# Batch 0 by quarters of the spectrum, `x` in rows of six, and one form of gate: a fused 2-D DFT and gated feed-forward on one Trainium2 core

## The chip, the cores and the metric

The kernel runs on one core of one Trainium2 chip. Five engines work from in-order queues of their own: TensorE (PE, with weight loads shown as PEld), VectorE (DVE), ScalarE (ACT), GpSimd (POOL) and SyncE (SP), which issues most transfers. The core has 16 DMA engines. The metric is the device time of one execution in microseconds (us); lower is better.

## The reference, cut to what matters

```
x: (8, 3008, 256) f32            # batch, sequence, channel
X = fft(fft(x, axis=1), axis=2).real          # (8, 3008, 256)
x = X.reshape(24064, 256)
gate = maximum(x @ w_gate, 0)                 # w_gate: (256, 1536)
val  = x @ w_val                              # w_val:  (256, 1536)
out  = (gate * val) @ w_out                   # w_out:  (1536, 256), out f32
```

## The kernel before

**The mathematics on the chip.** The transform along the channels is folded into the weights: `weights(c, ...)` multiplies cosine and sine tables (TA, TB) with `w_gate` (index 0) and `w_val` (index 1) and leaves WA, WB and WM in bf16, WM being WB with its mirror's sign and weight. The transform along the sequence is done for each batch as products with tables: tabC and tabS hold cosines and sines of six chunks of up to 128 sequence positions. By symmetry the input is first folded: row s is added to its mirror S - s with reversed channels (`fold_a`, `fold_a0`), the two halves of the sequence are added and subtracted (`fold_pq`, giving PQ, families 0 and 1), and the channels are folded to F (cosine part) and G (sine part) (`fold_f`, `fold_f0`, `fold_g`). XD holds rows in ascending order, XG their mirrors, which are gathered by index with indirect DMAs from POOL (`load_mirror`, six gathers of up to 128 pairs of rows); `load_rows` loads XD with six plain DMAs of 128 or 120 rows of two sequence positions, and two small ones. F and G times the tables give U and V, spectrum by columns: 4 x 376 + 1 columns for a batch.

**Feed-forward tiles.** A tile is one block of columns by 128 of the 1536 hidden features (12 tiles to a block). Both signs of the frequency come from the same U and V: WA and U plus WB and V give one sign, and adding WM and V gives its mirror. Each tile leaves h in bf16 for both signs, and blocks of h times `wo` give rows of the output (`out_steps`: for batches 1 to 7 96 products of 256 columns in each block), which go through ACT (os) to DRAM by DMAs from SP.

**Batch 0** is worked in four blocks ("segments") of 376 or 377 columns, and everything is set up around it: tables for odd frequencies on DVE and ACT, weights chunk 0, the fold of the batch on DVE (lines 303 to 312), the first transform `dft_first`, then the first block's 12 tiles (`first_tile`), with weights of chunks 1 and 2 between them, and then segments 1 to 3 (`single_tile`). POOL reduces the arguments of the even tables (`even_rest`), gathers batch 1's mirrors, and folds batches 1 and 2 (`fold_steps`, run before segments 2 and 3). The whole odd family (two segments) is transformed before the first tile, the even family during segment 1, and batch 1 in segments 2 and 3.

**Batches 1 to 7** have three blocks ("thirds") of 504, 504 and 497 columns, 36 slots to a batch (`slot`). While the tiles of batch b run, POOL folds batch b + 2, paced by a credit (`run_fold(fold_us)`, with costs written beside each step), and PE transforms batch b + 1 at slots written out by hand (`DFT_EVEN`, `DFT_ODD`). A tile is of one of two kinds. Kind "o" is computed with six products (two gate, gate mirror, two value, value mirror). Kind "n" takes five: the sine part of the gate in a product (`sine_part`, L689), copied out by ACT (L692); channel 128's share put into PSUM by ACT (`seed`, L684) and the cosine part added to it (`cosine_part`, L696); one sum on DVE (L700) and one on POOL (L701) give both signs. The rule is:

```python
st["kind"] = "o" if b < 6 and fi % (6 if b < 2 else 12) == 5 else "n"
```

which makes 6 tiles of batch 1 and 3 each of batches 2 to 5 of kind "o", 18 in all. Channel 128 of a batch goes through DRAM (`ch128`) and comes back by two DMAs on SP: `row_128` (all partitions of CB) and `row_0` (row 0 of V), queued with the transform's steps 6 and 21 in batch 0.

**Order.** Instructions are issued in the order in which the program emits them, each engine and each DMA queue in order; an instruction that waits holds what is behind it on its engine. DMAs from SP and ACT take eight semaphores in turn.

## Time and profile before

| | |
|---|---|
| median of 3 runs | 647.61 us (647.56 to 647.71) |
| the profiled execution | 647.91 us, its span 646.1 us |
| PE, PEld | 620.9 us (96%), 401.6 us (62%) busy |
| DVE, ACT, POOL | 543.7 us (84%), 450.6 us (70%), 535.5 us (83%) busy |
| first product on PE; first gate product | 16.0 us; 24.4 us |
| first output product of batch 1; of batch 2 | 113.3 us; 188.5 us |
| L701, POOL's sums for "n" tiles | 234 of 1252 ns |
| L102, gathers of mirrors | 48 of 1017 ns |
| granted clock of PE | 1.00 |

Times in the trace count from the span's start. A line L496 is line 496 of the kernel; a group "out<-in" names the tile written and those read. The share of busy time is a mean over stages with different limits, so stages are looked at one by one.

### The profile page before, as it was taken

The page shows a single profiled execution, that of the slowest core. Times are in us where ns is not written, and L with a number is a line of the kernel's source. Part 1 is how long each engine was busy: PE and PEld are TensorE (multiplying, and loading weights), DVE is VectorE, ACT ScalarE, POOL GpSimd, SP SyncE. Part 2 cuts the span into 40 slices and gives each one's busy share as a digit, 9 for nine tenths or more (in the row PEclk, how much of TensorE's full clock was granted, in tenths as well). Part 3 has the DMA queues.
Part 4 walks back from the last instruction along what each step waited for, and adds up shares of the span by engine and source line. Part 5 has one row for each costly group of instructions (what it writes and reads, how often), then busy time and mean ns, then how long its engine had stood idle before and what let it go on. Part 6 is the DMA issues. An engine that isn't in the chain of part 4 may idle for free.

```text
span 646.1 us, 12223 instructions
## 1 busy us (share of the span) xinstructions
PE 620.9 (96%) x4160; PEld 401.6 (62%) x4160; DVE 543.7 (84%) x970; ACT 450.6 (70%) x822; POOL 535.5 (83%) x593
## 2 busy tenths in 40 slices
PE   0999999999999999999999999999999999999996
PEld 0356676566666666666666666666666666666665
DVE  8875566887888899898998889988899899999990
ACT  8697666767666776777677677676777767777751
POOL 8589997899999999999899999999876656666660
PEclk9999999999999999999999999999999999999999
DMA  8922544224332433241222422311211111111112
GB/s 227 207 67 64 178 127 137 62 68 145 89 83 63 127 98 90 64 136 58 89 84 78 129 73 82 93 35 49 73 34 49 44 62 49 35 48 49 50 49 79
DMA packets 42438, 55.24 MB, mean 85 GB/s; under 512 B 5153, under 2 KB 32353, under 8 KB 42376
## 3 DMA queue, kind: packets, MB, share of 16 engines
q1 hardware_dynamic: 34552, 39.23, 19.7%
q0 software_dynamic: 7536, 14.72, 9.3%
q8 instruction: 32, 0.52, 0.4%
q10 hardware_dynamic: 288, 0.52, 0.2%
q14 instruction: 30, 0.25, 0.1%
HBM read 32.14 MB, written 24.67 MB: 88 GB/s over the span
## 4 chain that ended last, share of the span: by engine, by line
PE 69%; DVE 12%; POOL 9%; issue 6%; ACT 3%; DMA 0%; DVEq 0%; SPq 0%; ACTq 0%; POOLq 0%
PE o L496 27%; PE v L575 7%; PE v L570 7%; PE v L571 7%; DVE h L597 6%; PE g L689 5%; PE p L696 5%; DVE r L700 5%; POOL r L701 4%; PE d L385 4%; PE p L575 1%; POOL XG L113 1%; POOL PQ L121 1%; POOL XG L102 1%; PE p L571 1%
## 5 line engine op out<-in xcount | busy, mean ns | idle before, releaser
L701 POOL TENSOR_TENSOR r<-r 128x504 f32<-128x504 f32 (+1 forms) x234 | 291.7, 1252 | 73.8 <-DVE r L700 72.3
L496 PE MATMUL o<-wo,h 128*128 128x256 bf16 x2304 | 342.3, 273 | 0.0
L597 DVE SCALAR_TENSOR_TENSOR h<-r,v 128x504 bf16<-128x504 f32 (+1 forms) x468 | 297.3, 673 | 51.1 <-PE v L575 37.8
L496 PEld LDWEIGHTS <-h 128*128 128x128 bf16 x2304 | 225.2, 98 | 114.7 <-issue 2.3
L684 ACT ACTIVATE p<-CB,b 128x504 f32<-128x504 bf16 (+1 forms) x234 | 160.0, 684 | 55.3 <-DVE r L700 52.8
L692 ACT COPY r<-g 128x504 f32<-128x504 f32 (+1 forms) x234 | 135.0, 577 | 58.6 <-PE g L689 54.5
L700 DVE SCALAR_TENSOR_TENSOR r<-r,p 128x504 f32<-128x504 f32 (+1 forms) x234 | 156.7, 670 | 0.6 <-ACT r L692 0.6
L575 PE MATMUL v<-V,WM 128*128 128x504 bf16 (+3 forms) x296 | 108.6, 367 | 1.6 <-DVE h L597 1.0
L570 PE MATMUL v<-U,WA 128*128 128x504 bf16 (+3 forms) x296 | 108.6, 367 | 0.1
L571 PE MATMUL v<-V,WB 128*128 128x504 bf16 (+3 forms) x296 | 108.7, 367 | 0.0
L593 DVE TENSOR_TENSOR h<-r,v 128x376 bf16<-128x376 f32 (+3 forms) x124 | 68.9, 580 | 25.7 <-PE v L575 13.6
L689 PE MATMUL g<-V,WM 128*128 128x504 bf16 (+1 forms) x234 | 87.8, 375 | 0.5 <-ACT r L692 0.3
L696 PE MATMUL p<-U,WA 128*128 128x504 bf16 (+1 forms) x234 | 87.8, 375 | 0.0
L502 ACT COPY os<-o 128x512 f32<-128x512 f32 x96 | 55.7, 580 | 14.5 <-PE o L496 8.1
L570 PEld LDWEIGHTS <-WA 128*128 128x128 bf16 x366 | 35.7, 98 | 38.3 <-issue 8.9
L571 PEld LDWEIGHTS <-WB 128*128 128x128 bf16 x366 | 35.7, 98 | 35.7 <-ACT WB L291 0.7
L102 POOL DMA_INDIRECT XG<-in_x_dram,gidx x48 | 48.8, 1017 | 8.7 <-issue 6.3
L113 POOL TENSOR_TENSOR XG<-XG,XD 128x510 f32<-128x510 f32 x42 | 52.5, 1265 | 0.1
L585 ACT ACTIVATE r<-g 128x504 f32<-128x504 f32 (+3 forms) x48 | 27.3, 569 | 35.0 <-PE g L571 31.8
L585 ACT ACTIVATE r<-p 128x376 f32<-128x376 f32 (+1 forms) x80 | 38.2, 490 | 18.7 <-PE p L575 10.9
L121 POOL TENSOR_TENSOR PQ<-XG 128x510 f32<-128x510 f32 x42 | 45.0, 1091 | 0.0
L575 PEld LDWEIGHTS <-WM 128*128 128x128 bf16 x366 | 35.8, 98 | 11.4 <-issue 0.2
(127 smaller groups left out, 430.4 us busy)
## 6 DMA issues: line engine op xcount, KB each, us to landing
out_dram<-os SPq DMA_DIRECT2D x118, 128.0 KB
XD<-in_x_dram SPq DMA_DIRECT2D x30, 256.0 KB
out_dram<-os SPq DMA_DIRECT2D x62, 120.0 KB
XD<-in_x_dram SPq DMA_DIRECT2D x16, 240.0 KB
CB<-ch SPq DMA_DIRECT2D x7, 376.2 KB
out_dram<-os SPq DMA_DIRECT2D x10, 127.0 KB
XG<-in_x_dram,gidx POOLq DMA_INDIRECT x48
h<-in_moe_w_gate_dram POOLq DMA_DIRECT2D x3, 256.0 KB
```

The source lines that it names most:

```text
L496: nc.tensor.matmul(st["p"][:, q, :], lhsT=hs[f][:, sign, h0:h0 + 128], rhs=wo[:, f, :], start=(f == 0), stop=(f == NF - 1))
L570: nc.tensor.matmul(bank[:, 0:st["n"]], lhsT=WA[i][:, st["f"]], rhs=st["us"], start=True, stop=False)
L571: nc.tensor.matmul(bank[:, 0:st["n"]], lhsT=WB[i][:, st["f"]], rhs=st["vs"], start=False, stop=True)
L575: nc.tensor.matmul(bank[:, 0:st["n"]], lhsT=WM[i][:, st["f"]], rhs=st["vs"], start=False, stop=True, skip_group_check=True)
L593: nc.vector.tensor_tensor(half_h(st, sign), (r or st["r"])[:, 0:n], st["v"][:, 0:n], op=ALU.mult)
L597: nc.vector.scalar_tensor_tensor(half_h(st, sign), in0=st["s"][1 + sign][:, 0:n], scalar=0.0, in1=st["v"][:, 0:n], op0=ALU.max, op1=ALU.mult)
L684: nc.scalar.activation(st["p"][:, 0:st["n"]], st["c"], ACTF.Copy, scale=b2[:, st["fi"]:st["fi"] + 1])
L689: nc.tensor.matmul(st["g"][:, 0:n], lhsT=WM[0][:, st["f"]], rhs=st["vs"], start=True, stop=True)
L692: nc.scalar.copy(q[:, 0:n], st["g"][:, 0:n])
L696: nc.tensor.matmul(st["p"][:, 0:n], lhsT=WA[0][:, st["f"]], rhs=st["us"], start=False, stop=True, skip_group_check=True)
L700: nc.vector.scalar_tensor_tensor(sp[:, 0:n], in0=q[:, 0:n], scalar=-0.5, in1=st["p"][:, 0:n], op0=ALU.mult, op1=ALU.add)
L701: nc.gpsimd.tensor_tensor(sm[:, 0:n], sp[:, 0:n], q[:, 0:n], op=ALU.add)
```

## The change

Six things are changed together.

- **`x` in rows of six.** XD and XG hold six consecutive rows of `x` in a partition and use 126 partitions (NP): 125 with six rows each, and a last one filled by five small DMAs (`load_ends`; in batch 0 after a DMA of zeros to that partition). `load_rows` is two DMAs of 125 rows of 6 KB a batch (six DMAs of 125 rows of 2 KB in batch 0, three on SP's queue and three on ACT's), mirrors are two gathers of 125 rows of 6 KB instead of six. The fold now adds XG into XD, so XD is loaded for the next batch after `fold_pq` and not after `fold_a`; `fold_pq` takes all 256 channels at once.
- **Batch 0 in quarters.** Columns are ordered so that each block of 376 columns needs only 188 columns of the tables (`QUARTERS`). Before the first tile only quarter 0's tables are made and transformed; the tables of quarter 1 are reduced on POOL, of quarter 2 on POOL, of quarter 3 on DVE (`vector_rest`), the sines follow on ACT between the tiles, and each quarter is transformed during the block before it.
- **Fold of batch 0**: DVE does family 1 only; POOL does family 0 in `pool_goes_on`, called in the ninth tile of block 0, and then loads batch 1 and gathers its mirrors.
- **Weights** in four parts of 256, 384, 384 and 512 features (`PARTS`) instead of three of 512; WB is copied by DVE and WM of the last two parts made by POOL.
- **All tiles of batches 1 to 7 are of kind "n".** `run_fold` gets 0.8 in place of 1.1 (batch 1) or 0.9.
- **Order in batch 0**: the folds of batches 1 and 2 are queued from the eighth tile of block 1 at 2.0 a tile (`FOLD_0`); the transform of batch 1 is all in block 3, `row_128` with its step 6 and `row_0` with step 18.

```diff
-    ROWS = {0: (128, 128, 120), 1: (128, 128, 121)}
+    NP = 126
+    ROWS = {0: (NP, NP - 1, NP - 1), 1: (NP, NP, NP - 1)}
...
+    PARTS = ((0, 256), (256, 384), (640, 384), (1024, 512))
...
+    def load_rows(b, ts=slice(0, 3), queue=None):
+        o, (ks, _) = b * S * D, at(ts)
+        for r in range(2):
+            (queue if queue and r else nc.sync).dma_start(out=D6[0:NP - 1, r, ks],
+                                                         in_=dram(x, o + (1 + ks.start + r * H) * D, [[6 * D, NP - 1], [D, ks.stop - ks.start], [1, D]]))
+
+    def load_ends(b, own=True, mirror=True):
+
         o = b * S * D
...
+        last = slice(NP - 1, NP)
+        if own:
+            nc.sync.dma_start(out=D6[last, 0, 0:2], in_=dram(x, o + 751 * D, [[0, 1], [D, 2], [1, D]]))
+            nc.sync.dma_start(out=D6[last, 1, 0], in_=dram(x, o + (H + 751) * D, [[0, 1], [1, D]]))
+            nc.sync.dma_start(out=D6[last, :, 3], in_=dram(x, o, [[0, 1], [H * D, 2], [1, D]]))
+        if mirror:
+            nc.sync.dma_start(out=G6[last, 0, 4:6], in_=dram(x, o + (S - 752) * D, [[0, 1], [D, 2], [1, D]]))
+            nc.sync.dma_start(out=G6[last, 1, 5], in_=dram(x, o + (H - 751) * D, [[0, 1], [1, D]]))
...
+    def fold_a(e, p, r, ts):
+        ks, js = at(ts)
+        e.tensor_tensor(D6[p, r, ks, 1:D], D6[p, r, ks, 1:D], G6[p, r, js, D - 1:0:-1], op=ALU.add)
...
+    def fold_pq(e, p, i, ts):
+        ks, _ = at(ts)
+        e.tensor_tensor(P6[p, i, ks], D6[p, 0, ks], D6[p, 1, ks], op=SIGN[i])
...
         if b + 1 < B:
-            steps.append((0.0, lambda: load_rows(b + 1)))
-            gathers = [(1.3, lambda r=r, t=t: load_mirror(b + 1, t, r)) for t in range(3) for r in range(2)]
-        steps += [(1.1, lambda i=i, t=t: fold_pq(e, p, i, t)) for t in range(3) for i in range(2)]
...
+            steps += [(1.3, lambda r=r: load_mirror(b + 1, r)) for r in range(2)]
+        steps += [(1.1, lambda i=i, t=t: fold_pq(e, p, i, slice(t, t + 1))) for t in range(3) for i in range(2)]
+        if b + 1 < B:
+            steps.append((0.0, lambda: (load_rows(b + 1), load_ends(b + 1))))
...
+    HJ = NJ // 2
+    QUARTERS = [slice(NE, NE + HJ), slice(NE + HJ, NK), slice(0, HJ), slice(HJ, NE)]
...
+    load_rows(0, slice(0, 1), nc.scalar)
+    load_rows(0, slice(1, 2), nc.scalar)
+    load_rows(0, slice(2, 3), nc.scalar)
+    nc.vector.memset(zero[:], 0.0)
+    for X in (XD, XG):
+        nc.sync.dma_start(out=X[NP - 1:NP].rearrange("p r t q d -> p (r t q) d"), in_=zero[:].unsqueeze(1).to_broadcast([1, 12, D]))
+    load_ends(0)
...
+    for n in range(6):
+        w = space()
+        pool_rest(1, n, w[:, 0:HJ], w[:, HJ:2 * HJ])
...
+    def pool_goes_on():
+
+        for t in range(3):
+            fold_pq(nc.gpsimd, p, 0, tt[t])
+        load_rows(1)
+        load_ends(1)
+        for r in range(2):
+            load_mirror(1, r)
+        for part in (fold_f, fold_f0, fold_g):
+            part(nc.gpsimd, p, slice(0, 3), 0, 0)
...
+    for c, e, tiles_ in ((1, nc.vector, (0, 0, 1, 1)), (2, nc.gpsimd, (2, 2, 3, 3)), (3, nc.gpsimd, (4, 4, 5, 6))):
+        for fi, step in zip(tiles_, weights(c, (psO, "o", "o"), e)):
+            add_more(0, fi, step)
+    for n in range(6):
+        add_more(0, (3, 4, 6, 6, 7, 8)[n], lambda n=n: pool_rest(2, n, *(spare[:, k * HJ:(k + 1) * HJ] for k in (n, 6 + n % 2))))
+    add_more(0, 8, gate_128, pool_goes_on)
...
+    FOLD_0 = 2.0
+    DFT_0 = (0,) * 8 + (3, 3, 6, 0), (0,) * 7 + (3, 3, 3, 3, 0), (0,) * 7 + (3, 3, 3, 3, 1), (3,) * 8 + (0,) * 4
...
+    def folds():
+        for b in (1, 2):
+            todo_fold.extend(fold_steps(b))
+    add_more(1, 7, folds)
...
-                    st["kind"] = "o" if b < 6 and fi % (6 if b < 2 else 12) == 5 else "n"
+                    st["kind"] = "n"
...
-                for at, f in ((6 if b == 0 else 21, row_128), (21, row_0)):
-                    steps[at] = lambda step=steps[at], f=f: (f(), step())
+                for at_, f in ((6, row_128), (18, row_0)) if b == 0 else ((21, row_128), (21, row_0)):
+                    steps[at_] = lambda step=steps[at_], f=f: (f(), step())
```

## The prediction

> **What bounds the kernel now.** I read the windows by batch first, then the start as a timeline, then the DMA view of short windows, because the change touches how `x` is loaded. The windows (columns: length, then busy us of PE, PEld, DVE, ACT and POOL, granted clock, DMA share, GB/s) of batches 1, 4 and 6:

> ```profile
> 113.30:188.50 75.20, 74.65 (x488) 46.63 (x487) 63.65 (x110) 52.20 (x94) 71.31 (x78) 1.00 0.32 92
> 337.90:412.10 74.20, 74.20 (x496) 48.39 (x495) 66.36 (x115) 52.54 (x92) 70.71 (x77) 1.00 0.29 90
> 487.40:561.00 73.60, 73.60 (x493) 48.08 (x492) 67.75 (x117) 53.14 (x92) 44.99 (x37) 1.00 0.16 48
> ```

> PE is busy without a gap in batches 2 to 6 at clock 1.00: from 188 us on, a product less is time less. Batch 6 has no tile of the old kind "o" and batch 4 three; they differ by 0.6 us. POOL has some 3 us of slack in a batch.

> The start and the end of batch 0 are another matter. In lines of the timeline (start, length, engine, line, operation): DVE's first and last fold step for batch 0, the first gate product, and POOL waiting for the first tile of batch 1:

> ```profile
> 12.51 1.21 DVE L113 TENSOR_TENSOR XG<-XG,XD 128x1020 f32<-128x1020 f32 x1
> 22.35 0.42 DVE L137 TENSOR_TENSOR G<-PQ 121x254 bf16<-121x254 f32 x1
> 24.42 0.32 PE L570 MATMUL p<-U,WA 128*128 128x376 bf16 x1 [0.32 <-DVE U L402]
> 112.77 2.47 POOL L701 TENSOR_TENSOR r<-r 128x504 f32<-128x504 f32 x2 [3.78 <-DVE r L700]
> ```

> The fold ends at 22.8, the first gate starts 1.6 later, and the first output product of batch 1 is at 113.3. POOL is idle 3.8 us before its first sum for batch 1, so it is through with batch 2's fold in time. SP's queue in batch 0's last segment:

> ```profile
> 93.50 2.70 SPq L94 DMA_DIRECT2D XD<-in_x_dram  x6
> 96.24 1.24 SPq L98 DMA_DIRECT2D XD<-in_x_dram  x2
> 97.53 0.40 SPq L778 DMA_DIRECT2D CB<-ch  x1
> 99.73 0.24 SPq L781 DMA_DIRECT2D V<-ch  x1
> ```

> Row 0 of V (L781), which batch 1's first product reads, stands behind the loads of `x` for batch 3. That is harmless as long as those loads are quick.

> Last, two DMA windows: the first loads of `x`, of 128 rows each (2.6 to 5.0), and the middle of a store of 127 rows (567.2 to 569.2):

> ```profile
> q1 hardware_dynamic: 251, 0.46, 49.7%
> q10 hardware_dynamic: 228, 0.43, 47.4%
> ...
> DMA packets 48, 0.05 MB, mean 25 GB/s; under 512 B 0, under 2 KB 48, under 8 KB 48
> q1 hardware_dynamic: 48, 0.05, 6.9%
> ```

> The loads fill all 16 engines (97% over two queues); the 127-row store runs on one (6.9% of 16, 25 GB/s). The DMA records show more: one 4-byte packet per engine follows each transfer, 16 after 128 rows, 15 after 120, 11 after 121, 1 after 127. Each is the largest divisor up to 16 of the number of rows. The change loads 125 rows at a time (and one apart), so I count 5 engines.

> **Products saved.** 18 "o" tiles (6 in batch 1, 12 in 2 to 5) go from six products to five; one of 504 columns starts 0.212 us after the other: 18 x 0.212 = -3.8. POOL pays 1.25 for each (3.75 in a batch) and gets back four gathers (1.02 + 0.15 each, 4.7), six two-element sums (1.0) and two small ones (0.4): 70.7 - 2.3 = 68.4 of 73.6. The trace has no gather of 6 KB rows: between 1.0 us as now and 3.1 (three times the bytes) each; even that makes 72.6, below 73.6. I take 1.0, as the weight loads with twice as many descriptors take 0.75. ACT and DVE bear all-"n" tiles already in batch 6. Batch 1 loses 1.8 us now in waits behind POOL; half of that should go: -0.9 (0 to -1.8).

> **The start.** Half-width tables take less of DVE (0.41 + 0.36 + 0.61 at 376 columns; about 0.9 a chunk at 188, from the 129-column rows 0.28 + 0.23 + 0.35), so DVE could fold from 8.3 instead of 12.5. But the data come later. Six loads of 125 rows make 150 packets of 2 KB for each of 5 engines; a packet takes 84 ns in the trace: 12.6 us from 1.8, so 14.4. Two of six gathers may share these engines (2 us each): 14.4 to 18.5, I take 16.5. Behind them in the same rings lie the zeros for partition 125; the five loads of the ends write over them, so SP issues these only when the zeros have landed, 2 us for five (0.24 to 0.6 each in the rows) and 1.5 to land: 20. The first fold covers partition 125 and waits for all that. The fold itself: 2 x 1.2 + 0.1 + 2 x 0.61 + 0.1 + 2 x 0.34 + 2 x 0.33 = 5.0 for two thirds and 2.8 for the last, so it ends at 27.8 and the gate starts at 28.9, 4.5 later than now (bounds +1.5 and +8). If the rows spread over 16 engines: ends at 12.3, gate at 21.3, -3.1. Weights land in either case before that. [...]

> **Edits with one answer.** Rows of batch 0's output come in some ten more runs (0.25 to 0.45 us of SP each, and SP's queue is mostly idle); WB's copies go from ACT to DVE (six of some 0.5, counted in DVE's 17.2 below); three more space buffers only loosen a ring. I cost them at nothing; if DVE were full there, the copies would cost 3 us of batch 0, within its bounds.

> **Batch 0.** PE's stream from the first gate is 82.2 us now (taken: 88.1) and 84.5 after, as quarter 1's transform (18 x 0.08) and 0.85 of weight products move behind the gate. ACT's table steps alternate between two chunks, so that they overlap; in the first segment ACT and DVE (17.2 each) stand beside PE's 17.5. I take 91 in all, bounds 87 and 95: PE would be ready for batch 1 at about 120. But there it meets POOL and SP.

> POOL is released by the end of DVE's fold, 27.8. Twelve table reductions at 188 columns: 2.7 us each now at 377, between 1.5 and 2.1, I take 1.9, with four weight copies of 0.8: 26. Sum at 53.8. Three PQ for family 0: 57.1. Only then may batch 1's rows load, since the fold now adds into XD: 2 x 125 rows of 6 KB on 5 engines, 307 KB each at 24.4 GB/s = 12.6, with 1.3 for issue and landing: 71. POOL meanwhile gathers and makes F and G (6.4) and then waits to 71. Fold of batch 1 to its last PQ: 6 x 1.25 + 2 + 2.4 + 6.3 = 18.2, so 89.2. Batch 2's rows: 13.9 later, 103.1 (POOL's F and G end at 97). Fold of batch 2: last PQ at 121.3. What is late next is SP: `load_rows(3)` goes out in the fourth tile of the last segment, near 105, and waits there for that PQ until 121.3; queued behind it are the ends, output stores and `row_0` (step 18, seventh tile). `row_0` is issued near 124; one row means one engine, the lowest, whose ring then holds 12.4 us of rows: landed at 135. The 12th tile's `sine_part` reads row 0 of V, PE stands in order, and the first output product of batch 1 follows 2.5 later: 137.6 instead of 113.3, +24.3. In the later batches `row_0` precedes the loads by a slot or more, and a load has 13 slots before its fold: no cost, up to 1 us a batch.

> **Sum.** +24.3 - 3.8 - 0.9 = +19.6 on the profiled execution's 647.9 us (span 646.1 and 1.8 around it); against the median of 647.61 that is 667.2, say 667.

> **Rivals.** (1) The loads are no bottleneck: with 16 engines a batch's rows come in some 4 us. It decides where the rows land before POOL has made F and G (6.4 us after the issue). Then the gate is at 21.3, batch 0 takes 91 against 88.1, and -3.1 + 2.9 - 3.8 - 0.9 = -4.9: 642.7. For it: PE is at its limit later, so the 3.8 are sure. Against it: the counts 15, 11 and 1. It is also the case that the change does what it says. (2) The rows are slow, but `row_0` isn't caught (another engine, or SP gets to it earlier). Then POOL decides: batch 2's fold, all of it queued before batch 1's sums, ends at 121.3 + 7.6 = 129; its first sum comes 15 later than the 113 to 115 of now: +15 - 4.7 = +10, 658. For it: POOL runs in order; against: SP does too. (3) Gathers take the same five engines in turn and stretch both loads by up to 6 us: 679.

> **Chances.** The forecast 0.58, rival (2) 0.22, (3) 0.05, (1) 0.12, and 0.03 that losses and gains cancel. 0.2% is about what a measurement of this kernel can tell from no change. Range 651 to 681: the lower end is rival (2) with the start at its lower bound (+1.5 instead of +4.5) and POOL's reductions at 1.5 (another -4.8), the upper end is (3) with a little more. Rival (1) is left out.

> **What would show it.** Right: five engines busy in the first 15 us; the first DVE fold waiting for a DMA to near 20; SP waiting for a POOL PQ near 121; a gap of PE over 10 us before batch 1; then batches of 73.6 without "o". Wrong: DVE folding at 12 or earlier; POOL without waits for XD; the first L701 sum before 116.

## The result: 694.5 us in place of 647.7

The median of 6 runs is 694.48 us (693.56 to 695.32), that of the kernel before on the same chip 647.66 us (647.56 to 647.86): ratio 1.072, 95% interval 1.071 to 1.074. The forecast was 667, with a range of 651 to 681. The span of the profiled execution is 692.5 us against 646.1. The first output product of batch 1 starts at 160.6 us in place of 113.3 (+47.3), and everything behind it takes 517.2 us, up to the last tile of batch 7, in place of 517.8 (-0.6). So batch 0 holds the whole loss, and hardly any gain came back later.

### The profile page after: what moved, and what is told of

It is laid out like the page before. It is cut to its first block, busy times and chain, and to the rows that moved or that the text cites. A ratio compares the mean times of both kernels' runs of the same rounds, so it can differ in the third digit from the quotient of the medians.

```text
span 692.5 us, 12313 instructions
## 1 busy us (share of the span) xinstructions
PE 623.6 (90%) x4186; PEld 404.2 (58%) x4186; DVE 557.3 (80%) x1001; ACT 456.5 (66%) x863; POOL 545.6 (79%) x557
## 4 chain that ended last, share of the span: by engine, by line
PE 72%; POOL 12%; DMA 9%; DVE 3%; issue 2%; SPq 1%; ACT 0%; DVEq 0%; POOLq 0%; ACTq 0%
PE o L557 31%; PE v L659 8%; PE g L770 7%; PE p L777 7%; PE v L654 7%; PE v L655 7%; PE d L426 4%; DMA XG<-in_x_dram,gidx 3%; DMA XD<-zero 3%; POOL PQ L144 3%; POOL XD L134 2%; DMA V<-ch 2%; POOL XG L113 2%; DVE h L678 1%; POOL r L782 1%
## 5 line engine op out<-in xcount | busy, mean ns | idle before, releaser
L782 POOL TENSOR_TENSOR r<-r 128x504 f32<-128x504 f32 (+1 forms) x252 | 313.3, 1252 | 80.5 <-DVE r L781 77.8
L678 DVE SCALAR_TENSOR_TENSOR h<-r,v 128x504 bf16<-128x504 f32 (+1 forms) x504 | 318.4, 673 | 43.8 <-PE v L659 29.6
L765 ACT ACTIVATE p<-CB,b 128x504 f32<-128x504 bf16 (+1 forms) x252 | 172.4, 684 | 74.8 <-DVE r L781 72.9
L773 ACT COPY r<-g 128x504 f32<-128x504 f32 (+1 forms) x252 | 145.5, 577 | 93.3 <-PE g L770 88.5
L781 DVE SCALAR_TENSOR_TENSOR r<-r,p 128x504 f32<-128x504 f32 (+1 forms) x252 | 168.7, 669 | 24.2 <-ACT r L773 24.2
L770 PE MATMUL g<-V,WM 128*128 128x504 bf16 (+1 forms) x252 | 95.2, 378 | 22.9 <-DMA V<-ch 22.9
L134 POOL TENSOR_TENSOR XD<-XD,XG 126x510 f32<-126x510 f32 x42 | 52.9, 1270 | 22.6 <-DMA XG<-in_x_dram 14.8
L674 DVE TENSOR_TENSOR h<-r,v 128x376 bf16<-128x376 f32 (+1 forms) x88 | 44.9, 542 | 24.2 <-PE v L659 13.2
L144 POOL TENSOR_TENSOR PQ<-XD 126x512 f32<-126x512 f32 x45 | 56.6, 1269 | 0.0
L770 PEld LDWEIGHTS <-WM 128*128 128x128 bf16 x252 | 24.7, 98 | 29.8 <-DMA V<-ch 23.2
L659 PEld LDWEIGHTS <-WM 128*128 128x128 bf16 x348 | 34.2, 98 | 7.5 <-issue 0.3
L113 POOL DMA_INDIRECT XG<-in_x_dram,gidx x22 | 27.8, 1262 | 5.3 <-issue 4.9
```

The costliest lines, as they stand in the source:

```text
L144: e.tensor_tensor(P6[p, i, ks], D6[p, 0, ks], D6[p, 1, ks], op=SIGN[i])
L659: nc.tensor.matmul(bank[:, 0:st["n"]], lhsT=WM[i][:, st["f"]], rhs=st["vs"], start=False, stop=True, skip_group_check=True)
L678: nc.vector.scalar_tensor_tensor(half_h(st, sign), in0=st["s"][1 + sign][:, 0:n], scalar=0.0, in1=st["v"][:, 0:n], op0=ALU.max, op1=ALU.mult)
L765: nc.scalar.activation(st["p"][:, 0:st["n"]], st["c"], ACTF.Copy, scale=b2[:, st["fi"]:st["fi"] + 1])
L770: nc.tensor.matmul(st["g"][:, 0:n], lhsT=WM[0][:, st["f"]], rhs=st["vs"], start=True, stop=True)
L773: nc.scalar.copy(q[:, 0:n], st["g"][:, 0:n])
```

## The profile after

The windows of batches 1, 4 and 6 (columns as before the change: length, then PE, PEld, DVE, ACT, POOL, clock, DMA share, GB/s):

```profile
160.60:234.80 74.20, 73.75 (x481) 46.38 (x480) 66.56 (x116) 53.51 (x93) 68.75 (x67) 0.99 0.27 86
383.30:458.80 75.50, 73.86 (x493) 48.06 (x492) 67.91 (x117) 53.18 (x92) 71.90 (x70) 1.00 0.27 87
533.80:607.40 73.60, 73.60 (x493) 48.09 (x492) 67.73 (x117) 53.17 (x92) 45.04 (x37) 1.00 0.16 48
```

Batch 6, which had no tile of kind "o" before either, has kept its 73.6. Batch 4 is not shorter but longer (75.5 against 74.2): PE stands 1.6 us there. The same four events of the timeline as before the change:

```profile
27.70 2.35 DVE L134 TENSOR_TENSOR XD<-XD,XG 126x1020 f32<-126x1020 f32 x2 [19.81 <-DMA XG<-in_x_dram]
...
35.38 0.41 DVE L156 TENSOR_TENSOR G<-PQ 126x254 bf16<-126x254 f32 x1
...
36.96 0.47 PE L654 MATMUL p<-U,WA 128*128 128x376 bf16 x1 [0.21 <-ACT es L433]
...
159.53 2.55 POOL L782 TENSOR_TENSOR r<-r 128x504 f32<-128x504 f32 x2 [9.11 <-DVE r L781]
```

DVE's fold begins at 27.7 (12.5 before) after an idle time of 19.81 us that a DMA ended; the first gate is at 36.96 (24.42). SP's queue, at the start and where batch 1's row 0 is fetched:

```profile
1.96 0.87 SPq L213 DMA_DIRECT2D XD<-zero  x1
...
21.58 0.23 SPq L105 DMA_DIRECT2D XD<-in_x_dram  x1
...
142.98 0.66 SPq L97 DMA_DIRECT2D XD<-in_x_dram  x2
...
145.79 0.22 SPq L864 DMA_DIRECT2D V<-ch  x1
```

And the longest pieces of the chain that ended last in which it waits for a transfer (start, length, what):

```profile
1.96 19.54 DMA XD<-zero
...
23.29 4.10 DMA XG<-in_x_dram
...
68.29 21.49 DMA XG<-in_x_dram,gidx
...
145.79 11.69 DMA V<-ch
```

These four take 56.8 us. The last is the one that PE waits for, its longest wait of the whole execution (in the list of waits: engine, for whom, us in total, times, longest):

```profile
PE g L770 <- DMA V<-ch: 22.9, 1, 22.9
```

A DMA window in the middle of batch 1's load, 82 to 84 us, has the rows (q1) and a gather (q0) in it:

```profile
q0 software_dynamic: 23, 0.14, 16.4%
q1 hardware_dynamic: 23, 0.12, 14.6%
```

Together that is 31.0% of 16 engines, and 5 of 16 are 31.25%: what is left of both transfers here goes through the same five, each at half speed (23 packets each in 2 us, where the load of 125 rows alone has 43 in loads). The zeros at the start show the five too. They are twelve pieces of 1 KB, and in the trace their semaphore is counted up seven times by 4.1 us and five times from 19.4 to 21.5: seven pieces went through engines that were free, and five waited behind the rows.

## Experiments

Each kernel is compared with the kernel before on its chip; given are the median in us and the ratio with its 95% interval. loads, port and port2 leave the computation out and are one execution each; from them only the trace is read. Of the code only the lines that matter are shown, with ... between them.

**The transfers by themselves (loads).** 

> This kernel leaves the whole computation out: it only loads rows of 6 KB of x into SBUF, one load after another, each waiting until the one before has landed, with 128, 127, 126, 125, 124, 121, 120 and 112 rows by SP's queue; then 112 and 13 rows as two loads; then gathers of 128, 126, 125, 120 and 112 rows; then 125 rows and a gather of 125 rows together with one row queued behind them, and the same with 126. Theory A (the number of rows sets the number of engines, largest divisor up to 16, for plain loads and gathers alike; 84 ns for 2 KB, 2 us for issue and landing): 128 rows 4.0 us, 127 rows 34, 126 rows (14 engines) 4.3, 125 rows (5) 8.3, 124 rows (4) 9.8, 121 rows (11) 4.8, 120 rows (15) 4.0, 112 rows 3.8; 112 and 13 rows together 4.2; the gathers the same with up to 2 us more; 125 rows and a gather of 125 together 14 to 16, the single row behind them as late as the rows; with 126 some 7. Rival B (the load is slow through its 6 KB rows or its bytes, whatever their number): 112 to 128 rows all between 6 and 9 us. Rival C (plain loads follow the number of rows, but gathers are spread by descriptor over 16 engines): gathers of 125 rows as fast as of 128, and 125 rows beside a gather 8 to 10 us.

Measured, from a load's issue to the issue of the next one, which waits for it:

| rows of 6 KB | 128 | 127 | 126 | 125 | 124 | 121 | 120 | 112 | 112 + 13 |
|---|---|---|---|---|---|---|---|---|---|
| plain load, us | 4.5 | 31.9 | 5.0 | 7.9 | 11.4 | 6.4 | 5.6 | 4.8 | 6.2 |
| gather, us | 5.6 | - | 5.7 | 9.3 | - | - | 6.8 | 5.8 | - |

Windows inside the loads of 127, 125 and 112 rows and the gather of 125 (length, POOL busy, clock, DMA share, GB/s):

```profile
8.00:36.00 28.00, 0.00 (x0) 1.00 0.06 27
44.00:49.00 5.00, 0.00 (x0) 1.00 0.31 127
75.00:77.00 2.00, 0.00 (x0) 1.00 0.86 283
98.00:104.00 6.00, 0.00 (x0) 1.00 0.30 121
```

0.06 and 0.31 of 16 are 1 and 5 engines' worth, and the gather of 125 rows has 0.30. The load of 112 rows should use all 16 by theory A and has 0.86, 13.8 engines' worth; the trace has 16 of the 4-byte packets behind it. So the order of the times is that of theory A, for gathers too; B and C fall. The sizes fit less well: loads of 121, 120 and 124 rows took 1.6 us longer than reckoned, for in windows inside them they move 186, 206 and 84 GB/s on 0.64, 0.69 and 0.25 of the engines, which is about 340, 330 and 290 ns a packet (332 GB/s on 0.84 and 250 ns with 128 rows), and 112 and 13 rows as two loads took 6.2 in place of 4.2, only 1.7 less than 125 at once. The single row behind 125 rows was fetched 7.6 us after its issue, with the rows' last packets; behind 126 rows 3.7 us. Neither pair was together all along, as the gather went out 4.6 and 4.9 us ahead of the rows.

**Rows, gathers and row 0 of V, one after another.** The first kernel splits the rows of batches 1 to 7, the second also gathers 126 rows (14 engines by theory A) and sends the ends behind the gathers, the third only moves one DMA to another queue:

```diff
-            (queue if queue and r else nc.sync).dma_start(out=D6[0:NP - 1, r, ks], ...)
+            for p0, n in (((0, 112), (112, 13)) if b > 0 else ((0, NP - 1),)):
+                (queue if queue and r else nc.sync).dma_start(out=D6[p0:p0 + n, r, ks], ...)
...
-        gather(G6[0:NP - 1, r]...)
+        gather(G6[0:NP, r]..., NP)   # and, in load_ends, zeros again for three cells of partition 125
...
-                    nc.sync.dma_start(out=Vn[0:1, 0:4 * NJ + 1], in_=ch128[b + 1:b + 2, :])
+                    (nc.sync if b else nc.scalar).dma_start(out=Vn[0:1, 0:4 * NJ + 1], in_=ch128[b + 1:b + 2, :])
```

> The kernel after, with the loads of rows of batches 1 to 7 as 112 and 13 rows in place of 125; gathers and the start are as they were. Theory A (five engines): the rows land some 4 us after their issue, but the gathers still go through five engines, 12.6 us of packets: the fold of batch 1 begins near 82 instead of 88.1, that of batch 2 no longer waits (7.3 us now), SP's wait for the last difference of batch 2 ends near 130, row 0 of V lands near 135, first output product of batch 1 near 140 instead of 160.6: 674. Rival B (bytes, not the number of rows): 694, the fold of batch 1 still at 88.

Measured: 681.69, 1.051 (1.049 to 1.053). The fold of batch 1 begins at 85.1, the last difference of batch 2 is at 135.5, batch 1's first output product at 148.2. Splitting rows gains 12.8 us, which B had excluded, but not the 20 expected. The gathers, still of 125 rows (0.30 of the engines in loads), let the fold begin 3 us later than reckoned. And the split has a price of its own in SP's queue. A load is now nine transfers (four of rows, five of ends), the semaphores are eight in turn, and by the trace the ninth waits until the first has landed, 3.1 us in the last of these loads (139.4 to 142.5); row 0 of V stands behind it:

```profile
142.48 0.22 SPq L111 DMA_DIRECT2D XG<-in_x_dram  x1
143.21 0.22 SPq L865 DMA_DIRECT2D V<-ch  x1
```

It goes out 7.7 us after batch 2's last difference, where the kernel after takes 2.8.

> As the run before, and the gathers of batches 1 to 7 take 126 rows in place of 125 (the three cells that this overwrites in partition 125 are set to zero again by two small transfers of SP). Theory A: 14 engines; fold of batch 1 near 76, fold of batch 2 follows without a wait, last difference near 124, POOL is through near 131, before PE comes to batch 1 at 134: first output product near 136.5, 670. Rival C (gathers were never on five engines): no gain over the run before.

Measured: 679.23, 1.049 (1.047 to 1.051); first output product at 146.3, 2 us earlier than in the run before and 10 later than expected. Rows and gathers of batch 1 together (502 packets of 6 KB) still need 13.1 us, 67.4 to 80.5, which is 235 GB/s: on 14 or 16 engines by theory A, a packet takes 376 ns on the mean, in place of 234 for 125 rows alone. Then SP sets the cells to zero and sends the ends, and the fold begins at 83.9. Row 0 of V goes out 9.0 us after the last difference (132.6 to 141.6), again behind transfers that wait for the rows. How the miss divides between the two was not tried.

> The kernel after, with row 0 of V for batch 1 (L864) issued from ACT's queue in place of SP's; nothing else. Theory A: it is no longer behind SP's wait for the difference of batch 2 nor in the ring behind the rows, and lands before 137; then POOL decides, whose fold of batch 2 ends near 150.4: first output product of batch 1 near 152 instead of 160.6, 686. Rival D (only row 0 is late): first output product near 137, 671. Rival E (the single row is late through the five engines whatever its queue): no change, 694.

Measured: 684.22, 1.056 (1.054 to 1.058). The first output product is already at 138.8, as in rival D, but batch 1's first block then takes 35.5 us in place of 25, because POOL's fold of batch 2 ends at 151.8: PE waits 7.7 us of it for that fold. The next late thing is POOL, at the price of theory A.

**The start.**

```diff
+    nc.vector.memset(zero[:], 0.0)
+    for X in (XD, XG):
+        nc.sync.dma_start(out=X[NP - 1:NP]..., in_=zero...)   # ahead of the rows
     load_rows(0, slice(0, 1), nc.scalar)
...
```

> The kernel after, with the zeros for partition 125 written ahead of batch 0's rows in place of behind them; nothing else. Theory A: the zeros land near 4, the ends are issued at once and land behind the rows of the lowest engine near 20, so DVE folds from 20.5 (second pair of mirrors 21.5) in place of 27.7; all that follows moves by about 7: 687.5. Rival F: the ends come last whatever precedes them, held by the weights in 16 to 32 us: 694.

Measured: 691.05, 1.067 (1.064 to 1.070). The ends go out at 6.8 to 14.6, the fold begins at 22.55 in place of 27.7 and the first gate is at 31.8; it is now the mirrors that DVE waits for. 5.1 us at the gate are 4.1 us at batch 1.

> Batch 0's start alone: zeros first, its rows as loads of 112 and 13 rows (16 and 13 engines) and its gathers of 126 rows (14 engines; three cells of partition 125 are set to zero again behind them); batches 1 to 7 as in the kernel after. Theory A: rows and mirrors (3 MB) land near 14, at the 245 GB/s that the last run's rows and gathers reached together, the small transfers behind them near 17; fold from 17, 8 us as in the kernel after, first gate near 27 (36.96 now): 684.5. Rival: the fold ends no earlier than the tables and weights let PE begin, gate near 30: 687.5.

Measured: 689.25, 1.063 (1.061 to 1.065); fold from 18.4, gate at 27.8, batch 1 begins 7.7 us earlier than in the kernel after. Of the 12.5 us that the start had lost, the number of engines and the place of the zeros make 9.2.

**All of these together.**

> Start, rows and gathers of all batches and row 0 of V together (the edits of start16, rows16_gather14 and row0_act). Theory A: POOL, released 10 us earlier, waits 4 us less for batch 2's rows than now and ends its fold of batch 2 near 130; it decides, since PE would be ready near 124: 662.5. If POOL is not the bound: 659. Rival: the gains are one and the same wait and don't add: 674 or more. The kernel before's 647.6 is not reached in any of these, because the start is still 2.5 us later and batch 0's tiles 8 us longer.

Measured: 662.55, 1.021 (1.019 to 1.024). PE's first output product of batch 1 is at 126.3, POOL's fold of batch 2 ends at 131.2, and PE stands 2.9 us in batch 1's first slots. The gains add up, and POOL is what is late next.

**Kind n alone, in the kernel before.**

```diff
-                    st["kind"] = "o" if b < 6 and fi % (6 if b < 2 else 12) == 5 else "n"
+                    st["kind"] = "n"
...
-                    pending = slot(cur, *ahead, per_tile, 1.1 if b == 1 else .9)
+                    pending = slot(cur, *ahead, per_tile, 1.1 if b == 1 else .95)
```

> The kernel before with one part of the change alone: all tiles of batches 1 to 7 of kind n (five products), fold credit 0.95. If PE's products decide: 18 products less, 644. If POOL decides: it gets 3.75 us more in batches 2 to 5 (71 and 72 of 74 now) and 7.5 in batch 1, and has none of the relief that fewer gathers give: 74.5 a batch against PE's 73.5, and batch 1 some 4 us longer: 649.

Measured: 660.32, 1.019 (1.017 to 1.021). Batches 1 and 2 take 79.7 and 79.8 us in place of 75.2 and 74.1, with POOL busy for 73.8 and 78.2 of them. POOL decides, and it costs more than I had reckoned: in the kernel before, the "o" tiles were POOL's relief.

**Batch 1's loads earlier.**

```diff
-    def pool_goes_on():
+    def pool_loads():
         for t in range(3):
             fold_pq(nc.gpsimd, p, 0, tt[t])
         load_rows(1)
...
+    def pool_goes_on():
         for part in (fold_f, fold_f0, fold_g):
...
+    add_more(0, 6, pool_loads)
```

> The kernel after, with one move: the three differences of family 0, the loads of batch 1's rows and ends and its gathers are issued in block 0's seventh tile, ahead of four of the table reductions on POOL, in place of behind them in the ninth tile. Theory A (POOL's wait for batch 1's rows and mirrors is on the path that ends in row 0 of V): the loads go out 8 us earlier, the fold of batch 1 begins near 80 in place of 88.1, and all to row 0 of V moves by 8: 686.5. Rival: the earlier loads delay reductions that ACT's tables and PE wait for, 692 or more.

Measured: 686.65, 1.061 (1.058 to 1.064). The fold of batch 1 begins at 79.5, batch 1 at 152.9: the wait of 14.8 us for batch 1's mirrors was on the path.

> The same move on top of the kernel with start, rows, gathers and row 0 of V mended (662.5). Theory A: POOL's wait of 11.5 us for batch 1's rows shrinks by 8, its fold of batch 2 ends near 123 in place of 131.2, before PE comes to batch 1; the 3.05 us stall in batch 1's first slots and the half clock behind it (1.7) go: 658. Rival G (POOL is not what batch 1 waits for): 662.5.

Measured: 667.08, 1.029 (1.027 to 1.031): slower than without the move. Block 2 takes 32.1 us in place of 23.7. DVE and POOL in the timeline of this kernel:

```profile
77.93 7.87 DVE L254 TENSOR_SCALAR r<-r 128x189 f32<-128x189 f32 x1
85.72 0.40 DVE L257 SCALAR_TENSOR_TENSOR r<-kvec,u,r 128x189 f32<-128x189 f32 x1
...
78.33 7.35 POOL L149 TENSOR_TENSOR PQ<-XD 126x512 f32<-126x512 f32 x6
```

An instruction that takes 0.25 us elsewhere takes 7.87, to the end of POOL's six differences at 85.7; what stands behind it on DVE, PE's tiles first, waits. The same is in the kernel after, less long: an L246 of 0.30 us took 4.28 from 69.13 on, to the end of POOL's F and G at 73.3, and PE stood 2.7 us.

> As all_early, and DVE's argument reductions for quarter 3 begin in block 1's seventh tile in place of its first, so that none meets POOL's unbroken F and G of batch 0 (in the last kernel one such instruction, 0.4 us by itself, took 3.09 us there, to the end of POOL's G, and PE stood 2.15). Theory H (DVE's instruction is held by POOL's): all of L257 and L251 near 0.3 to 0.5 us, PE's 2.15 gone: 656. Rival (the stretch comes with the instruction, wherever it stands): a 3 us instruction elsewhere, 658.

Measured: 666.23, 1.028 (1.026 to 1.030). In block 1 no reduction takes more than 1.5 us, but in block 2 an L254 at 79.7 took 7.71 us, again to the end of POOL's six differences. The meeting that costs most stayed, 2 us later. The run does not tell H from its rival; port and all_early_q3 do.

> As all_early_late, but with the tiles of kind o and the fold credits of the kernel before: 18 tiles with six products in place of five. If PE decides in batches 1 to 5: 0.5 us more in each of batches 2 to 5 and 1.0 in batch 1, 659. If POOL decides (as where the kernel before was given kind n alone): no loss or a gain, 654 to 656.

Measured: 670.92, 1.036 (1.034 to 1.037). With the "o" tiles, and the fold credits that went with them, batches 1 to 5 are longer by 2.2, 0.6, 1.0, 0.8 and 0.6 us: in the changed frame kind "n" is worth 4.7 us (670.92 - 666.23).

**DVE beside POOL.**

> This kernel leaves the whole computation out. DVE runs four kinds of instruction, each first with POOL at rest and then while POOL runs three sums of two SBUF operands (126x768) without a break, and again while POOL runs eight short one-operand instructions: (a) one operand in SBUF, 128x189 (as L246), (b) two operands in SBUF, 128x189 (as L252), (c) one in SBUF and one in PSUM, 128x376 (as L674), (d) one in PSUM, 128x189. Theory H: (a) and (b) take 0.3 to 0.45 us at rest and stand to the end of POOL's three sums (up to 5 us) in company; (c) and (d) are as at rest. Rival (DVE's stretch comes from something else, such as transfers): all four as at rest.

```profile
7.86 5.57 POOL L56 TENSOR_TENSOR C<-A,B 126x768 f32<-126x768 f32 x3
...
8.52 1.26 DVE L43 TENSOR_SCALAR r<-k,sc 128x189 f32<-128x189 f32 x1
...
33.18 0.31 DVE L43 TENSOR_SCALAR r<-k,sc 128x189 f32<-128x189 f32 x1
```

Measured: (a) 1.26 us beside POOL's sums, 0.31 beside its one-operand instructions; (b) 1.27 and 0.41; (c) and (d) 0.55 and 0.41, as at rest. So DVE is held, by kinds as H says, but to the end of one of POOL's sums (9.7), not of three.

> As port (the computation is left out again), but the three sums of POOL write three tiles in place of one, so that none waits for the one before and POOL goes from one to the next without letting go, as in its fold. Theory H, in the form that port leaves (DVE gets in only where POOL stops between two instructions): (a) and (b), begun some 0.7 us after POOL's first sum, take about 4.7 us, to the end of the third; (c) and (d) as at rest. Rival (one POOL instruction is all that DVE ever waits for): 1.26 us again.

Measured: 1.26 and 1.34 us again. That POOL's sums follow without a gap is not what holds DVE over several of them. What does in the kernel stays open.

**Quarter 3's reductions at the start, where DVE waits for x anyway.**

```diff
+    m3 = single("m3", [128, 6, NE - HJ])
...
+    reduced([(m3[:, n], kvec[:, QUARTERS[3]], ...) for n, c in enumerate(order)])
...
-        add_more(1 + i // 12, i % 12, vector_rest(n, part))
```

> The kernel after, with quarter 3's argument reductions on DVE moved from blocks 1 and 2 to the start, where DVE waits for x (two space buffers fewer to make room). Theory H: no DVE instruction is held by POOL any more, block 1 loses its stall of 2.7 us and the half clock behind it (1.3), so block 1 is 22 instead of 26.3; but the time stays at 694, since row 0 of V decides when batch 1 begins. If batch 0's tiles were on the path: 690.

Measured: 695.33, 1.073 (1.072 to 1.075). Block 1 takes 22.2 in place of 26.3, and batch 1 begins at 161.2 (160.6 in the kernel after): in the kernel after, the meeting of DVE and POOL is real, but hidden behind row 0 of V.

> The same move on top of the kernel with start, rows, gathers and row 0 of V mended (662.5). Theory H and POOL as the next bound: PE comes to batch 1 some 3.5 us earlier, but POOL's first sum stays at 131, and the stall there grows by as much: 662. If POOL was not the bound: 659.

Measured: 662.57, 1.022 (1.020 to 1.024): PE comes to batch 1 at 124.3 in place of 126.3, and batch 1 takes 79.2 in place of 77.7: it waits for POOL instead.

> The same move on top of all_early (667.1). Theory H: the 7.87 us instruction of DVE in block 2 and PE's 9 us behind it are gone, SP's queue moves on, batch 2's rows land near 96 in place of 104, POOL is through with its fold near 123, when PE comes to batch 1: 655.6. Rival (block 2 stood for another reason, as late loads or tables): 663 or more.

Measured: 655.67, 1.011 (1.010 to 1.013). No DVE instruction of batch 0's tiles takes more than 0.68 us, blocks 1 and 2 take 22.8 and 22.7, batch 1 begins at 123.4, and the clock stays at 1.00. With this theory H stands in the form that the two meet and that their meeting costs what was reckoned; what keeps DVE waiting over several of POOL's instructions is not shown. But for 0.3 us in the next run this is as fast as the changed kernel got; no version of it beat the kernel before.

**PE's rate at the start.**

```diff
+    warm = psD.tile([128, 512], F32, name="d", tag="d")
+    for _ in range(110):
+        nc.tensor.matmul(warm[:, 0:HJ], lhsT=tabS[0:NP, 1, QUARTERS[0]][:, 0:128], rhs=tabS[0:NP, 1, QUARTERS[0]], start=True, stop=True)
```

> As all_early_q3 (655.7), with 110 products more on PE ahead of the first weights (a table times itself, into a bank that nobody reads), from 5.7 us on, so that PE is busy before its first real work. Theory K (PE works at half rate until it has been busy some 5 us, which the granted clock does not show at the start: products of 376 columns are 0.31 us apart until 33 us and 0.16 after): it is at full rate from about 11 us, the first gate comes 0.5 earlier and block 0 is 2.6 us shorter: 652.6. Rival (the slow products come from late operands): 655.7.

Measured: 655.33, 1.012 (1.010 to 1.013): no gain. PE was at full rate from 11.7 us (the first 40 of the 110 products take 6.4 us, the other 70 5.6), but had only 1.2 us of work in the 3.9 before 21.9, and the first tiles ran at half rate again, 0.31 us apart:

```profile
12.00:18.00 6.00, 5.60 (x70) 5.46 (x68) 2.58 (x13) 1.66 (x10) 5.69 (x7) 1.00 0.76 175
18.00:21.90 3.90, 1.21 (x8) 0.60 (x7) 3.30 (x5) 2.05 (x6) 3.75 (x7) 1.00 1.16 153
22.00:27.80 5.80, 3.76 (x18) 1.22 (x18) 5.18 (x16) 0.62 (x2) 0.93 (x3) 0.50 1.30 195
27.90:32.00 4.10, 3.93 (x13) 1.71 (x14) 2.18 (x5) 1.41 (x4) 3.61 (x9) 0.50 0.79 107
```

So the half rate here comes with a granted clock of 0.50 and not with late operands, and the remedy failed: the full rate did not last through the gaps that follow.

## Why the prediction was right in kind and 27 us short

The direction and the chain were right: five engines, the ends behind the zeros, POOL waiting for rows, SP waiting for batch 2's last difference, row 0 behind both and behind the rows in the ring. What failed are sizes, of three terms: the start, put at +4.5 and measured at +12.5; batch 1's load, put at 13.9 and measured at 21.6; and the gain behind batch 1, put at 4.7 and measured at 0.6. The links up to batch 1, as forecast and as measured (us from the span's start):

| link | forecast | measured | the link's own excess |
|---|---|---|---|
| batch 0's fold ends, POOL released | 27.8 | 35.9 | +8.1 |
| POOL's reductions and weight copies | 53.8 | 62.7 | +0.8 |
| differences of family 0 | 57.1 | 66.5 | +0.5 |
| batch 1's rows and mirrors landed, fold begins | 71.0 | 88.1 | +7.7 |
| last difference of batch 1 | 89.2 | 108.5 | +2.2 |
| batch 2's rows landed, fold begins | 103.1 | 123.2 | +0.8 |
| last difference of batch 2 | 121.3 | 143.0 | +1.6 |
| row 0 of V issued; landed | 124; 135 | 145.8; 157.5 | +0.1; +0.7 |
| first output product of batch 1 | 137.6 | 160.6 | +0.5 |

The excesses make the 23.0 us between forecast and measurement at batch 1. The start and batch 1's load hold 15.8 of them. Of the rest, POOL's sums for P and Q hold most: forecast at 1.05 to 1.1 us each as in the kernel before (1.09 on the mean), they take 1.27 now that each has all 256 channels, fifteen of them on this path. That a single row goes to the lowest engine, as the forecast's step to 135 and the expectation of zeros_first have it, no run shows; what the runs showed in its place is row 0 of V landing 11.7 us after its issue in the kernel after, and in loads a single row 7.6 us after its issue behind 125 rows and 3.7 behind 126.

**The start (forecast +4.5, bounds +1.5 and +8, measured +12.5).** The step "two of six gathers may share these engines" was too small: the rows landed at 21.1 and the zeros behind them at 21.5, not at 16.5. The trace has gathers and, from 14 us on, weights moving beside the rows all that time. "1.5 to land" for the ends was 4.1, because "weights land in either case before that" was wrong: POOL's weight loads had to wait for gathers (idle times of 0.9, 2.3 and 3.2 us before them), ran until 33 us, and filled the engines when the ends came (POOL's queue has 96.8% of 16 engines from 20 to 34 us). zeros_first and start16 show both halves. The upper bound of +8 did not allow for either.

**Batch 1's load (forecast 13.9, measured 21.6).** I costed the rows and left the mirrors out; they are as many bytes and also on five engines. That is rival (3), which I gave 5% and put at 679; its place was right, its size (6 us) nearly so for batch 1 (+7.7), but not for batch 2 (+0.8), whose gathers go out 9 us ahead of its rows. It was the forecast's own chain with that term in it. The shares changed on the way: at 72 to 74 us the rows' queue and the gathers' have 24.8% and 40.0% of the engines (10.4 in all), at 82 to 84 14.6% and 16.4% (5), which fits gathers that lie in part on the rows' five engines and in part on five others. Which engines a gather takes is not shown.

**Batch 0's tiles (forecast 91, bounds 87 and 95, measured 97.5 from the gate to the end of the last tile).** Three things were missing: DVE held by POOL (2.7 us in block 1, and a clock of 0.50 from 73.6 to 77.0 behind it), PE's half rate in the first 2.5 us (products of 376 columns 0.31 us apart in place of 0.16), and a wait of 2.1 us for POOL's late G. PE's busy time itself, reckoned at 82.2 before and 84.5 after, is 86.3 and 89.8 in the windows. All this cost nothing here (q3 shows it for block 1), since row 0 came later than PE in any case. In all_early it is on the path, and taking the first of the three away brings 11.4 us (667.08 to 655.67). What holds the mended version above 647.6 is a gate 3.7 us later and block 0, which takes 24.0 us in place of 18.0. How the latter divides between the low rate, the weights' two more passes and ACT was not separated.

What holds DVE is shown by kinds alone: in port, instructions whose operands are all in SBUF took 1.26 and 1.27 us beside POOL's sums of two operands, to the end of one sum, against 0.31 and 0.41 beside its one-operand instructions, and those with an operand in PSUM 0.55 and 0.41 beside the sums. The kernel's 3.1 (all), 4.3 (after) and 7.9 us (all_early), over several of POOL's instructions, are longer, and no run shows why.

**Products saved (-3.8 and -0.9 forecast).** Measured as a term by itself the 18 tiles are worth 4.7 us, as forecast in sum. That the tail gained only 0.6 has other causes: with the "o" tiles, the mended kernel's batches 1 to 5 are 2.4 us longer than the kernel before's (75.6, 74.2, 75.8, 75.5, 75.4 against 75.2, 74.1, 75.3, 74.2, 75.3). Batch 4 is the largest part, since POOL there has four gathers (three for `b == B - 1`), DVE waits 1.7 us for POOL's sums, and PE stands 1.6 us behind DVE; in all_early_late, with 126 rows to a gather instead of 125, the batch is 0.8 us shorter (74.7 against 75.5). "No cost, up to 1 us a batch" was too kind by about half a microsecond a batch, and POOL's busy time in batch 2 is 70.4 and not the 68.4 reckoned, again through the sums for P and Q and gathers of 1.2 us. And batch 1 began at half clock: PE had stood for 22.9 us, and its clock (third column from the end) came back only at 162.3:

```profile
134.00:138.00 4.00, 0.62 (x5) 0.27 (x3) 1.01 (x2) 0.57 (x2) 3.67 (x4) 1.00 0.36 105
138.00:142.00 4.00, 0.00 (x0) 0.00 (x0) 0.00 (x0) 0.00 (x0) 4.00 (x5) 0.56 0.59 221
...
158.50:160.00 1.50, 1.50 (x6) 0.56 (x4) 0.68 (x1) 1.32 (x4) 0.47 (x1) 0.50 0.07 17
...
164.00:168.00 4.00, 4.00 (x28) 2.43 (x26) 3.42 (x7) 2.83 (x6) 2.66 (x3) 1.00 0.12 34
```

**Rivals.** (1), 16 engines, is out (loads). (2), row 0 not caught and POOL in its place, is what row0_act made: it gains 10.3 us, so POOL's limit lay 10 us below row 0's, near the 8.6 of the forecast (137.6 against 129). The price of (2), 658, is not what row0_act measures, since the start and batch 1's load are late there as well. The lower end of the range, worked out from its own terms (658 - 3.0 - 4.8), is 650 and not 651; nothing hung on it.

## What to carry to other kernels

Choose the number of rows of a transfer by its divisors: 125 rows took 1.6 times as long as 126, plain or gathered, and 127 rows 6.4 times, and a short transfer queued behind them pays too (7.6 us behind 125 rows, 3.7 behind 126). Follow the bytes of a load that shares its engines, mirrors included, and ask of each small transfer what lies in its queue and on its engine. After a change, look at lone long instructions: one of 0.25 us that took 7.9 showed where DVE and POOL met, which no busy share does.
